# Reworking the ending of a fused state-space and attention kernel: earlier output sums, preloaded banks, a hinted branch

## The chip, the cores and the metric

One core of a Trainium2 chip, not the same chip on every occasion; every ratio compares kernels run on one chip in the same rounds. The metric is the device time of one execution in microseconds (us). Ratios are the mean time of one kernel's runs over the mean of the other's of the same rounds, so not quite the ratio of the medians that are quoted beside them. The brackets are 95% intervals.

Engines: PE is the TensorE matmul, PEld its weight load, DVE is VectorE, ACT is ScalarE, POOL is GpSimd, SP is SyncE (it issues nearly all DMAs: 167 of the 170 issues that the page of the kernel before lists, ACT the other 3).

## The reference, cut to what matters

The output is a gated mix of a complex diagonal state-space layer and 32-head attention on the same input, 2048 tokens of 1024 channels, in bf16:

```python
g = _sigmoid((x * gate_w).sum(-1, keepdims=True))
a = _A_ref(x, ...)          # h[t] = Lam_bar*h[t-1] + Bu[t];  y = 2*Re(h C) + x*Dskip
b = _B_ref(x, wqkv, wo)     # softmax(q k / sqrt(32)) v, all 32 heads, then @ wo
return g * a + (1 - g) * b
```

## The kernel before: the parts that the change touches

A scheduler in the program lays out 512 bursts. A burst computes scores (QK, 8 matmuls), gives them to two exps of 128x1024 on ACT, accumulates PV (16 matmuls) for the burst two before it, and fills the rest of PE's time with up to four matmuls of "dense" work (projections, state-space sums). Eight bursts make a unit of 256 query rows (two tiles of 128) and four heads; eight units make a head group. In the last group (bursts 448 to 511) the dense work is the output projection: 32 sums of 128x512. Each is added to a finished state-space tile, which was parked in DRAM (`ag_scratch`) and is loaded back into eight slots `Al` that reuse the memory of the input x.

```python
# the last group's sums: four partial ones of the last 256 rows, then the full ones
self.a_order = [28, 29, 30, 31] + list(range(28))
outs = [(2, self.d_out(7, r, cb, 2 * r + cb, range(7), fin=False)) for r in range(2) for cb in range(2)]
for qb in range(7):
    ...                                         # ready at burst 8*qb + 10 of the group
    outs.append((8 * qb + 10, self.d_out(qb, r, cb, k, [0, 1, 2, 3, 4, 5, 6, 7])))

for p in range(NBURST + 2):
    if p < NBURST: self.burst(p)
    if p >= 2:     self.pv(p - 2)
    ...
    if p == 448:                                # dense work has been done since burst 441
        ...                                     # load wo, part 3
        for k in range(8): ...                  # load Al[0..7] from ag_scratch

def d_out(...):                                 # sum in PSUM bank 7, then on DVE:
    scalar_tensor_tensor(o, ps[:, bank, :], gc, al, ALU.mult, ALU.add)

def tail(self):                                 # after the DMA transpose of the last unit
    for r in range(2):
        for cb in range(2):                     # one matmul and one DVE addition each
            matmul(ps[:, bank, :], OT[:, 7, ...], wo[7]..., start=True, stop=True)
            scalar_tensor_tensor(o, ps[:, bank, :], gcol, self.part[2*r+cb], mult, add)
        self.st_out(14 + r, r)
    ...                                         # range check of all 64 units, flag matmul, flag copy

def stream(name, e):                            # on each of the five engines
    S.emit(name, e, sems)                       # the whole fast path
    e.wait_ge(<flag written>)
    e.reg_load(r, flag[0:1, 0:1])
    with e.If_ne(r, 0):                         # the general path, never taken with these inputs
        ...
```

Every engine's list is one sequence, and in the traces a matmul that waits holds up the matmuls behind it. PSUM (`ps` in the code, declared as 128x8x512 f32) is what the matmuls write; one of its eight 128x512 tiles is called a bank here.

## Time and profile before

| | before |
|---|---|
| median of 3 runs, lowest to highest | 984.54 us, 984.47 to 985.25 |
| span of the profiled execution | 984.5 us (its own time: 987.31 us) |
| busy: ACT / PE / DVE | 96% / 92% / 53% |

The profiled execution is thus 2.8 us slower than the median.

From the profile page of the kernel before: busy tenths of PE and ACT in 40 slices of 24.6 us, the granted PE clock in the same slices, and the chain of work that ended last as shares of the span by engine.

```profile
span 984.5 us, 33446 instructions
...
PE   8889999999999999999999999999999999789995
...
ACT  3789999999999999999999999999999999999994
...
PEclk9999999999999999999999999999999999699998
...
ACT 88%; DVE 5%; PE 4%; DMA 2%; SPq 0%; issue 0%
```

ACT bounds the kernel: the exps hold 88% of the chain. What can be gained in the ending is what stops the exps there, and what stands after the last of them. The slice with clock 6 is around 850 us.

The timeline of ACT alone, kernel before, from 780 us on (start, duration, instructions in a row without a gap over the view's threshold; in brackets the idle time before the group and what ended it):

```profile
779.48 77.33 ACT L1431 ACTIVATE f_pt<-f_ps 128x1024 bf16<-128x1024 f32 x84
857.60 1.94 ACT L1431 ACTIVATE f_pt<-f_ps 128x1024 bf16<-128x1024 f32 x2 [0.80 <-PE f_ps L1425]
859.93 14.77 ACT L1431 ACTIVATE f_pt<-f_ps 128x1024 bf16<-128x1024 f32 x16 [0.39 <-PE f_ps L1425]
875.14 95.70 ACT L1431 ACTIVATE f_pt<-f_ps 128x1024 bf16<-128x1024 f32 x104 [0.44 <-PE f_ps L1425]
```

The exps pause at 857.6 and 859.9 because PE's scores (L1425) are late. Why they are late is seen in the windows of the same kernel (busy time of each engine and its number of instructions, then the granted clock, the DMA share and GB/s):

```profile
839.20:842.60 3.40, 1.80 (x48) 1.17 (x48) 0.02 (x2) 3.40 (x5) 0.00 (x0) 1.00 0.29 80
842.60:859.70 17.10, 12.48 (x206) 6.03 (x207) 0.91 (x4) 16.14 (x18) 0.00 (x0) 0.50 0.39 132
```

With no dense work PE was busy for 1.80 of 3.40 us, then its clock was halved for 17.1 us (column PEclk: 0.50). In the clock records every stretch at one clock that ends within the span is a multiple of 3.41 us: at half clock 3.41 (the shortest, at 13.17 us before) and 17.07 us (this one). So the clock is laid out below in windows of 3.4 us. PE was not idle in the one just before the drop: it was busy for 53% of it (1.80 of 3.40 us).

The chain of waits of the kernel before, from the last exps on (start, duration, what):

```profile
958.00 12.84 ACT f_pt L1431 x14
...
970.89 0.38 PE f_ps L1447 x8
...
971.29 0.22 DVE f_rc L1460
...
972.00 2.28 DMA f_OT<-f_On
...
974.32 0.40 PE f_ps L1641
...
974.75 1.14 DVE f_xT L1646 x2
...
976.07 1.40 DVE f_xT L1646 x2
...
979.15 0.18 PE f_ps L1664
979.33 0.02 issue
979.35 0.15 DVE flag L1666
```

After the last exp (970.83): last PV, reciprocal, a DMA transpose of 2.28 us, four matmuls and four additions one after another, the range check, the flag at 979.50. The view ends there, since branches aren't counted as work. The trace's records go on: a compare-and-branch at 980.03 to 980.11 on every engine, the next instruction of any engine only at 983.63 to 984.00, and instruction-fetch DMAs that start at 980.95 to 981.14 in between; then the closing barrier to 984.53. The last output store had landed at 979.51.

### The profile page before, as it was taken

To read this page: it belongs to the slowest core of one execution; us is meant where nothing else is said; L and a number is where in the kernel's file an instruction comes from. 1 tells how busy PE (TensorE), PEld (TensorE's weight loads), DVE (VectorE), ACT (ScalarE), POOL (GpSimd) and SP (SyncE) were. 2 spreads that over 40 slices of the span, in tenths; PEclk is the share of its full clock that TensorE was granted. 3 is DMA by queue.
4 is the path that set the end of the run, shared out by engine and by line. 5 is a ranking of instruction groups with operands and counts; after the bars stand their busy time and mean duration, and the time that the engine had idled before them with its cause. 6 is when DMAs were issued, how large, how long until landed. Compare 5 with 4: busy or idle time off the path is not lost.

```text
span 984.5 us, 33446 instructions
## 1 busy us (share of the span) xinstructions
PE 908.1 (92%) x15204; PEld 490.7 (50%) x15426; DVE 518.6 (53%) x1193; ACT 943.3 (96%) x1030; POOL 8.4 (1%) x46
## 2 busy tenths in 40 slices
PE   8889999999999999999999999999999999789995
PEld 5544554554444464444645544445544456344442
DVE  4897889877778844411267711187753112122223
ACT  3789999999999999999999999999999999999994
POOL 2000000000000000000000000000000000000000
PEclk9999999999999999999999999999999999699998
DMA  9982312311135202120023111152101210334321
GB/s 208 182 133 51 42 24 50 62 26 39 41 68 103 50 5 50 38 71 29 19 37 82 30 35 41 39 91 49 29 7 48 82 50 5 104 89 124 104 79 64
DMA packets 157302, 60.99 MB, mean 62 GB/s; under 512 B 145888, under 2 KB 145888, under 8 KB 157152
## 3 DMA queue, kind: packets, MB, share of 16 engines
q1 hardware_dynamic: 153952, 57.96, 26.8%
q8 instruction: 123, 2.02, 0.9%
q10 hardware_dynamic: 3200, 0.80, 0.4%
q14 instruction: 27, 0.22, 0.1%
HBM read 16.79 MB, written 12.58 MB: 30 GB/s over the span
## 4 chain that ended last, share of the span: by engine, by line
ACT 88%; DVE 5%; PE 4%; DMA 2%; SPq 0%; issue 0%
ACT f_pt L1431 88%; PE f_ps L1301 1%; DMA f_OT<-f_On 1%; DVE f_OT L1206 1%; PE f_ps L1425 1%; DVE f_OT L1202 1%; PE f_ps L1447 1%; DVE f_OT L1204 1%; DMA f_xT<-in_A_x_dram 1%; PE f_ps L1386 1%; SPq L1008 0%; DVE f_OT L1203 0%; PE f_ps L1283 0%; DVE f_V L1307 0%; PE f_ps L1332 0%
## 5 line engine op out<-in xcount | busy, mean ns | idle before, releaser
L1431 ACT ACTIVATE f_pt<-f_ps 128x1024 bf16<-128x1024 f32 x1024 | 941.0, 1251 | 16.9 <-PE f_ps L1425 16.8
L1447 PEld LDWEIGHTS f_ps<-f_V,f_pt 128*128 128x128 bf16 x8192 | 239.1, 96 | 111.2 <-issue 106.8
L1447 PE MATMUL f_ps<-f_V,f_pt 128*128 128x33 bf16 x8192 | 291.6, 178 | 0.8 <-DVE f_On L1461 0.5
L1425 PE MATMUL f_ps<-f_Q,f_K 32*128 32x256 bf16 x4096 | 206.0, 276 | 26.3 <-ACT f_pt L1431 8.2
L1425 PEld LDWEIGHTS f_ps<-f_Q,f_K 32*128 32x128 bf16 x4096 | 61.0, 92 | 241.7 <-ACT f_pt L1431 233.0
L1332 PE MATMUL f_ps<-f_xT,f_wb 128*128 128x512 bf16 x448 | 117.2, 377 | 13.6 <-DVE f_Q L1290 2.4
L1283 PE MATMUL f_ps<-f_xT,f_wb 128*128 128x512 bf16 x434 | 113.6, 379 | 9.0 <-issue 2.1
L1371 DVE TENSOR_SCALAR f_Ag<-f_ps,f_gcol 128x512 f32<-128x512 f32 x32 | 24.0, 751 | 139.8 <-PE f_ps L1356 139.8
L1232 DVE TENSOR_TENSOR_SCAN f_ht<-f_pf,f_init,f_ut 128x512 bf16<-128x512 f32 x64 | 80.4, 1273 | 0.0
L1356 PE MATMUL f_ps<-f_cT_im,f_hp 128*128 128x512 bf16 x192 | 72.6, 378 | 6.0 <-DVE f_Ag L1371 2.9
L1336 DVE CAST f_ub<-f_ps 128x512 bf16<-128x512 f32 x64 | 44.2, 691 | 51.9 <-PE f_ps L1332 51.8
L1301 PE MATMUL f_ps<-f_wb,f_xT 128*128 128x128 bf16 x1024 | 68.6, 222 | 0.0
L1386 PE MATMUL f_ps<-f_wb,f_OT 128*128 128x512 bf16 x220 | 59.3, 385 | 5.9 <-DVE f_xT L1396 2.0
L1301 PEld LDWEIGHTS f_ps<-f_wb,f_xT 128*128 128x128 bf16 x1024 | 59.1, 99 | 0.4 <-issue 0.2
L1332 PEld LDWEIGHTS f_ps<-f_xT,f_wb 128*128 128x128 bf16 x512 | 40.5, 96 | 35.9 <-issue 4.3
L1283 PEld LDWEIGHTS f_ps<-f_xT,f_wb 128*128 128x128 bf16 x496 | 39.2, 96 | 34.5 <-issue 1.4
L1396 DVE SCALAR_TENSOR_TENSOR f_xT<-f_ps,f_gcol,f_xT 128x512 bf16<-128x512 f32 x28 | 21.0, 751 | 64.6 <-PE f_ps L1386 64.6
L1356 PE MATMUL f_ps<-f_cT_re,f_hp 128*128 128x512 bf16 x144 | 54.4, 378 | 0.0
L1290 DVE CAST f_Q<-f_ps 128x512 bf16<-128x512 f32 x31 | 21.4, 691 | 51.3 <-PE f_ps L1283 51.3
L1223 DVE TENSOR_TENSOR f_tq<-f_ub,f_Et 128x512 bf16<-128x512 bf16 x128 | 46.3, 418 | 0.1
L1223 DVE TENSOR_TENSOR f_tq<-f_ht,f_Et 128x512 bf16<-128x512 bf16 x128 | 46.3, 417 | 0.0
L1307 DVE CAST f_V<-f_ps 128x512 bf16<-128x512 f32 x32 | 22.2, 694 | 43.2 <-PE f_ps L1301 43.2
(102 smaller groups left out, 420.1 us busy)
## 6 DMA issues: line engine op xcount, KB each, us to landing
ag_scratch<-f_Ag SPq DMA_DIRECT2D x32, 256.0 KB, 2.0
f_xT<-ag_scratch SPq DMA_DIRECT2D x32, 256.0 KB, 2.7
f_wb<-in_B_wqkv_dram SPq DMA_DIRECT2D x21, 256.0 KB, 4.2
out_dram<-f_xT SPq DMA_DIRECT2D x16, 256.0 KB, 2.3
f_OT<-f_On SPq DMA_TRANSPOSE x64, 2.4
f_wb<-in_B_wo_dram SPq DMA_DIRECT2D x1, 1024.0 KB
f_wb<-in_B_wqkv_dram ACTq DMA_DIRECT2D x3, 256.0 KB, 4.4
f_wb<-in_B_wo_dram SPq DMA_DIRECT2D x1, 768.0 KB, 4.9
```

What stands on the lines that cost most here:

```text
L1223: ops.append((c, lambda: dve(lambda e: e.tensor_tensor(o, a, b, op), r, w)))
L1232: ops.append((1.25, lambda ri=ri: dve(lambda e: e.tensor_tensor_scan(ht[:, ri, :], rr, ut[:, ri, :], self.init[:, ri, j:j + 1], ALU.mult, ...
L1283: mms.append((1, lambda e, f, l, a=a: e.matmul(ps[:, bank, :], w[:, g % 2, part, a, :], xT[:, a, 512 * ch:512 * (ch + 1)], start=f, stop=l ...
L1301: m = e.matmul(ps[:, bank, 128 * q:128 * (q + 1)], xT[:, a, 128 * kt:128 * (kt + 1)], w[:, g % 2, 2, a, :], start=(a == 0), stop=(a == 7))
L1332: mms.append((1, lambda e, f, l, a=a: e.matmul(ps[:, 7, :], bT[:, n % 2, ri, a, :], xT[:, a, 512 * ch:512 * (ch + 1)], start=f, stop=l), [ ...
L1336: self.dve(lambda e: e.tensor_copy(self.ub[:, n % 2, ri, :], ps[:, 7, :]), [("bank", 7)], [("ub", n % 2, ri)], "evac_u")
L1356: mms.append((1, lambda e, f, l, j=j, ri=ri: e.matmul(ps[:, 7, :], hp[:, ri, j, cols], cT[ri][:, j, 512 * cb:512 * (cb + 1)], start=f, sto ...
L1371: self.dve(lambda e: e.tensor_scalar(a, ps[:, 7, :], self.gcol[:, 0, tt:tt + 1], None, ALU.mult), [("bank", 7), "g0"], [at], "evac_c")
L1386: mms.append((1, lambda e, f, l, j=j: e.matmul(ps[:, bank, :], OT[:, j, 256 * qb + 128 * r:256 * qb + 128 * (r + 1)], wo[j][0][:, 512 * cb ...
L1425: m = e.matmul(ps[:, 2 * sl[h // 2] + h % 2, 256 * kl:256 * (kl + 1)], K[32 * h:32 * h + 32, g % 2, 128 * kt:128 * (kt + 1)], Q[32 * h:32 ...
L1431: self.act(lambda e, s=s, p=p: e.activation(pt[:, p], ps[:, 2 * s:2 * s + 2, :], ACT.Exp, scale=SCALE), [("S", s)], [("pt", p)], "exp")
L1447: m = e.matmul(ps[:, 6, o:o + 33], pt[:, p, h2, 256 * kl + 128 * qt:256 * kl + 128 * (qt + 1)], V[:, g % 2, 2 * i + kl, h, :], start=(i == ...
```

## The change

Intent: start the output projection as soon as the dense work runs out (burst 442), so that the clock isn't dropped; make the end after the last exp short: no DMA transpose, no serial additions, most of the check done earlier, and no instruction fetch behind the branch. A branch hint is an instruction of its own, placed some way ahead of the branch that it belongs to.

```diff
+        rcb = [(r, cb) for r in range(2) for cb in range(2)]
+        seq = [(442, 6, r, cb, "part") for r, cb in rcb] + [(450, 7, r, cb, "part") for r, cb in rcb]
+        for qb in range(6):
+            seq += [(458 + 8 * qb, qb, r, cb, "full") for r, cb in rcb]
+        seq += [(506, 6, r, cb, "rest") for r, cb in rcb]
...
-        for p in range(NBURST + 2):
+        for p in range(NBURST):
...
-            if p == 448:
+            if g >= 6 and not last and not proj[7] and not us and not cs and cur is None and not self.bg:
+                last = True                     # loads of wo part 3 and of Al[0..7] follow
...     # partial sums of the last 256 rows are kept as a bf16 pair hi + lo
+            if kind == "part" and qb == 7:
+                add(su, al, alt, ...); tensor_copy(hi, su); tensor_tensor(lo, su, hi, ALU.subtract)
...     # tail: put them back into PSUM by identity matmuls, and let the last product add to them
+        check(0, 63, 0, 63, 0)
+        self.pv(NBURST - 2)
+        preload(0)
+        self.pv(NBURST - 1, (0,))
+        preload(1)
+        self.pv(NBURST - 1, (1,))
+        ...     # reciprocal; two halves normalised, transposed on PE, copied by ACT
+        check(63, 64, 63, 65, 2)
+        ...     # 4 tail matmuls with start=False, the flag matmul after the first two
+        ...     # plain copies to bf16, two on ACT and two on DVE, and two stores
...
+    MARK_AT = dict(pe=64, act=24, dve=40, pool=1, sp=16)    # operations before the end of the stream
...
-                with e.If_ne(r, 0):
+                br = e.br_cmp(r, 0, on_true="done_" + name, on_false="bad_" + name, comp_op="IS_EQ")
+                br.branch_hint(loc[0])          # loc: marked MARK_AT operations before the end
```

## The prediction

> **What bounds it now.** ScalarE's exp stream: by the chain that ended last it holds 88% of the span; 1024 exps start 0.914 us apart (instructions in order of time), waiting for PE only 16.8 us in all (the waits). The change touches none of that. It aims at the 13.7 us from the end of the last exp (970.84) to the end of the span (984.5). In order of time these are: last PV, reciprocal, normalise (to 971.98); a DMA transpose of 2.3 us to 974.3; four tail matmuls feeding four 0.74 us DVE additions in a row (to 977.47); the check and flag, 2.0 us, to 979.50; register load 0.5 us; a compare-and-branch after which no engine does anything for 3.5 us (980.09 to 983.6, with two instruction-fetch DMAs inside it); then semaphore waits and the closing barrier, 0.9 us. The last output store had landed by about 979.2, so everything after that is flag and branch.
>
> A second loss: between bursts 441 and 449 PE has no dense work (838 to 855 us, PE 50 to 70% busy by stretches) and its clock is granted only 0.5 from 842.6 to 859.7. The first output sums then run at half clock and the exps lose 1.2 us in idle, 1.7 us by the spacing of their starts.
>
> **What changes.**
> 1. Partial sums start at burst 442 instead of 450. The dense gap shrinks to one period, so this clock drop should vanish: -1.7 us. But the first sum must wait for its scratch load, which landed around 843.7; PE has almost no slack before the next QK: about +0.4.
> 2. Last unit: the DMA transpose (2.3) becomes two PE transposes and two ScalarE copies of 128x128 (estimate 0.3 each from 0.60 for 128x512 and 0.20 for 128x8), pipelined with a split normalise: about 1.2.
> 3. The four additions become two ScalarE and two DVE copies in parallel.
> 4. Check: 63 of 64 units are checked early, but the short remainder (about 1.2 us of 0.16 to 0.3 us pieces) precedes DVE's copies, and the flag matmul stands before the last two tail matmuls.
> 5. The store becomes last (1.7 us from issue to landing), overlapped with register load and branch.
> 6. Branch hint: the 3.5 us should fall to some 0.1. [...]
> 7. Cost: eight 512-column preload matmuls stand among the last PVs; at 0.215 us each the second four delay the last PV by about 0.4 us.
>
> **The risk.** From burst 507 to 511 PE carries one dense matmul per burst or none. [...] in this trace mere 50% occupancy did it. I expect the half clock again (chance 0.7), and then preloads and tail take twice as long: about +2.3 us.
>
> **Sum.** With the clock whole, last exp to end is about 7.3 us instead of 13.7: -6.4; mid-kernel -1.2: 976.9. With the half clock 979.3. Hint failing: up to +2.5, chance 0.15. Mean about 978.5. Range 975.8 to 981.5. Faster by over 2% (under 965) is out of reach: 0.01; slower 0.005.
>
> **What would show it.** No half clock and no ScalarE idle at 842 to 860; branch under 0.3 us on all engines; no DMA transpose after the last exp; matmul spacing of the preloads 0.215 or 0.43 us; last to land is the final output store; last exp about 1.2 us earlier.
>
> **What would make it wrong.** The hint not taking, or hurting the straight instruction stream; [...] the first sums stalling exps more; late transposes at bursts 459 and 491 (now 0.4 us each) growing.

Three passages are cut from it, because no trace of this case shows what they say: what makes a branch stall, what makes the clock halve ("did it", in what is left of "The risk", means that the clock halved: after the window with PE busy for 1.80 of 3.40 us), and an item of the last list that presumes a threshold of the clock. 984.5 - 6.4 - 1.2 is the 976.9, and 2.3 more for the half clock the 979.3 (979.2 by the rounded terms). Two figures are estimates: the 0.1 us of step 6 (in the trace before the compare-and-branch records of ACT, DVE, POOL and SP last 0.05 to 0.07 us, and the 3.5 us stand behind them), and the 2.3 us of the half clock (matmuls of 512 columns start 0.215 us apart there at whole clock and 0.43 at half).

## The result, and the profile after

| first set, same chip | before | after |
|---|---|---|
| median, lowest to highest | 984.50 us, 983.89 to 985.25 (4 runs) | 982.49 us, 980.73 to 983.78 (4 runs) |
| ratio | | 0.9978 [0.9960, 0.9996] |

The change is a little faster, and 1.0 us outside the predicted range. Repeated on another chip (run e5 below) the ratio was 0.9955.

The page of the kernel after, the same rows as before:

```profile
span 982.1 us, 33717 instructions
...
PE   7889999999999999999999999999999999899996
...
ACT  4789999999999999999999999999999999899996
...
PEclk9999999999999999999999999999999999899997
...
ACT 87%; PE 5%; DVE 5%; DMA 1%; SPq 1%; issue 0%; DVEq 0%
```

The low clock in the 35th slice is nearly gone, but ACT has lost a tenth in that very slice. To see the sums, the two spans are cut at the same exps (times of starts, from the records of the two traces):

| stretch | before, us | after, us | difference |
|---|---|---|---|
| start to exp 64 (code unchanged) | 87.69 | 85.88 | -1.81 |
| exp 64 to 832 (bursts 32 to 416, unchanged) | 704.64 | 704.62 | -0.02 |
| exp 832 to 1008 (bursts 416 to 504) | 163.46 | 165.74 | +2.28 |
| exp 1008 to end of the last | 15.05 | 15.31 | +0.26 |
| last exp to end of span | 13.70 | 10.50 | -3.20 |
| span | 984.53 | 982.06 | -2.47 |

The start-up difference is put down to the run and not to the change: the code there is the same, and it lies between 85.6 and 87.7 us in the profiles told here. So in these two profiles the change bought 3.2 us at the end and gave 2.5 us back before it.

ACT's timeline after, from 780 us on:

```profile
779.54 64.44 ACT L1447 ACTIVATE f_pt<-f_ps 128x1024 bf16<-128x1024 f32 x70
847.65 1.94 ACT L1447 ACTIVATE f_pt<-f_ps 128x1024 bf16<-128x1024 f32 x2 [3.66 <-PE f_ps L1441]
850.04 112.04 ACT L1447 ACTIVATE f_pt<-f_ps 128x1024 bf16<-128x1024 f32 x122 [0.46 <-PE f_ps L1441]
962.29 9.27 ACT L1447 ACTIVATE f_pt<-f_ps 128x1024 bf16<-128x1024 f32 x10 [0.21 <-PE f_ps L1441]
```

The small pauses of before are gone, but there is one of 3.66 us at 847.65, when the first output sums run. All engines in that stretch of the kernel after, cut to the lines that matter:

```profile
839.27 4.71 SPq L1572 DMA_DIRECT2D f_xT<-ag_scratch  x8
...
844.35 0.75 DVE L1401 SCALAR_TENSOR_TENSOR f_xT<-f_ps,f_gcol,f_xT 128x512 f32<-128x512 f32 x1 [6.95 <-DMA f_xT<-ag_scratch]
...
845.16 1.89 PE L1395 MATMUL f_ps<-f_wb,f_OT 128*128 128x512 bf16 x4 [2.97 <-DVE f_xT L1401]
...
846.98 0.61 PE L1441 MATMUL f_ps<-f_Q,f_K 32*128 32x256 bf16 x8
```

Read it downwards. The load of the first state-space tile is issued at 839.27 (SPq). The first sum is ready long before, but its addition on DVE starts only at 844.35, released by that load. The second sum needs the same PSUM bank, so its first matmul stands on PE for 2.97 us, and the scores of the next burst (L1441) stand behind it in PE's order until 846.98. ACT has nothing to do in the meantime.

The windows of the kernel after: around this pause, and around the second drop of the clock.

```profile
841.80:848.60 6.80, 3.83 (x46) 1.59 (x43) 0.75 (x1) 3.14 (x5) 0.00 (x0) 0.63 0.91 302
959.70:963.10 3.40, 2.15 (x46) 1.24 (x42) 1.16 (x2) 3.19 (x4) 0.00 (x0) 1.00 0.32 101
963.10:972.00 8.90, 7.58 (x119) 3.68 (x119) 3.44 (x9) 8.46 (x10) 0.00 (x0) 0.50 0.16 61
```

In the first, the mean clock is 0.63: half clock for 6.83 us from 843.61, a result of the pause (PE was busy for 1.71 us of the 3.40 before it; in e3, without the pause, the clock stays whole there). In the last, half clock from 963.08 for 10.24 us: bursts 506 to 511 have one dense matmul or none. The chain of waits of the kernel after, from there:

```profile
970.50 1.71 PE f_ps L1665 x4
972.21 0.23 PE f_ps L1463 x8
972.44 1.36 PE f_ps L1665 x4
973.80 0.21 PE f_ps L1463 x8
...
974.03 0.22 DVE f_rc L1675
974.25 0.02 issue
974.27 0.37 DVE f_On L1678 x2
...
974.69 0.24 PE f_ps L1681
...
974.96 0.29 ACT f_OT L1684
...
976.54 0.14 DVE flag L1704
```

The eight preload matmuls (L1665) stand between the last PVs (L1463), so the reciprocal starts at 974.03, 2.47 us after the last exp (971.56); before it was 0.46 us. From the reciprocal to the flag it takes 2.65 us (before: 8.2), as meant. The rest is in the records of branches, fetches and landings:

| after the flag, us after the last exp | before | after |
|---|---|---|
| flag written | 8.67 | 5.12 |
| last store issued | 6.67 | 5.79 |
| last of its 16 parts landed (us after its issue) | 8.68 (2.01) | 9.63 (3.84) |
| branch to next instruction: PE | 3.54 | 0.55 |
| the same: ACT / DVE / POOL / SP | 3.87 / 3.89 / 3.77 / 3.63 | 2.66 / 3.65 / 3.33 / 2.90 |
| SP past its branch | 12.84 | 9.62 |
| end of span | 13.70 | 10.50 |

Two things were unexpected. Only PE's branch became short; an 8 KB instruction fetch for each of the other four still ran about 1 us after its branch. And the last store became slow: 12 of its 16 parts landed within 2.04 us of the issue, the other four after 2.53, 2.90, 3.58 and 3.84 us, while these fetches ran. The store's end (981.19) and SP's next instruction (981.18) came at the same moment.

One thing the profile doesn't cover: the reported time is longer than the span, by 1.7 to 1.8 us in all runs of the kernel after, but by 2.8, 3.5 and 3.3 us (means of 11 runs on each later occasion) in those of before. So part of the gain lies after the span's end. In the profile of before one more instruction fetch is recorded 2.7 us after the end of the span; the one of after has none. The same went together in e1 and e6 below (fetch 2.0 and 2.2 us after the end, differences of 2.46 and 2.28 us), and e12, without hints but without such a fetch either, has 1.75. The two go together in the profiles; as a cause it was not isolated.

### The profile page after: what moved, and what is told of

Same layout as the page of the kernel before. It is cut to its first block, busy times and chain, and to the rows that moved or that the text cites. A ratio compares the mean times of both kernels' runs of the same rounds, so it can differ in the third digit from the quotient of the medians.

```text
span 982.1 us, 33717 instructions
## 1 busy us (share of the span) xinstructions
PE 938.0 (96%) x15436; PEld 489.8 (50%) x15436; DVE 524.9 (53%) x1210; ACT 944.9 (96%) x1034; POOL 8.4 (1%) x46
## 4 chain that ended last, share of the span: by engine, by line
ACT 87%; PE 5%; DVE 5%; DMA 1%; SPq 1%; issue 0%; DVEq 0%
ACT f_pt L1447 87%; PE f_ps L1463 1%; PE f_ps L1395 1%; PE f_ps L1441 1%; DVE f_OT L1214 1%; PE f_ps L1309 1%; DVE f_OT L1210 1%; DVE f_OT L1212 1%; DMA f_xT<-ag_scratch 1%; SPq L1016 0%; PE f_ps L1291 0%; DVE f_OT L1211 0%; DMA f_xT<-in_A_x_dram 0%; PE f_ps L1340 0%; DVE f_V L1315 0%
## 5 line engine op out<-in xcount | busy, mean ns | idle before, releaser
L1463 PEld LDWEIGHTS f_ps<-f_V,f_pt 128*128 128x128 bf16 x8192 | 239.7, 96 | 110.5 <-issue 106.4
L1463 PE MATMUL f_ps<-f_V,f_pt 128*128 128x33 bf16 x8192 | 291.9, 179 | 0.5 <-DVE f_On L1477 0.5
L1441 PE MATMUL f_ps<-f_Q,f_K 32*128 32x256 bf16 x4096 | 205.2, 275 | 23.1 <-ACT f_pt L1447 4.9
L1441 PEld LDWEIGHTS f_ps<-f_Q,f_K 32*128 32x128 bf16 x4096 | 61.0, 93 | 240.9 <-ACT f_pt L1447 231.5
L1340 PE MATMUL f_ps<-f_xT,f_wb 128*128 128x512 bf16 x512 | 131.0, 378 | 4.1 <-DVE f_Q L1298 2.4
L1291 PE MATMUL f_ps<-f_xT,f_wb 128*128 128x512 bf16 x496 | 127.4, 380 | 2.3 <-DVE f_V L1315 1.3
L1364 PE MATMUL f_ps<-f_cT_re,f_hp 128*128 128x512 bf16 x192 | 72.8, 379 | 0.3
L1395 PE MATMUL f_ps<-f_wb,f_OT 128*128 128x512 bf16 x252 | 67.9, 388 | 4.7 <-DVE f_xT L1401 3.0
L1401 DVE SCALAR_TENSOR_TENSOR f_xT<-f_ps,f_gcol,f_xT 128x512 bf16<-128x512 f32 (+1 forms) x32 | 24.0, 751 | 71.5 <-PE f_ps L1395 64.5
```

The costliest lines, as they stand in the source:

```text
L1291: mms.append((1, lambda e, f, l, a=a: e.matmul(ps[:, bank, :], w[:, g % 2, part, a, :], xT[:, a, 512 * ch:512 * (ch + 1)], start=f, stop=l ...
L1340: mms.append((1, lambda e, f, l, a=a: e.matmul(ps[:, 7, :], bT[:, n % 2, ri, a, :], xT[:, a, 512 * ch:512 * (ch + 1)], start=f, stop=l), [ ...
L1364: mms.append((1, lambda e, f, l, j=j, ri=ri: e.matmul(ps[:, 7, :], hp[:, ri, j, cols], cT[ri][:, j, 512 * cb:512 * (cb + 1)], start=f, sto ...
L1395: mms.append((1, lambda e, f, l, j=j: e.matmul(ps[:, 7, :], OT[:, j, 256 * qb + 128 * r:256 * qb + 128 * (r + 1)], wo[j][0][:, 512 * cb:51 ...
L1441: m = e.matmul(ps[:, 2 * sl[h // 2] + h % 2, 256 * kl:256 * (kl + 1)], K[32 * h:32 * h + 32, g % 2, 128 * kt:128 * (kt + 1)], Q[32 * h:32 ...
L1463: m = e.matmul(ps[:, 6, o:o + 33], pt[:, p, h2, 256 * kl + 128 * qt:256 * kl + 128 * (qt + 1)], V[:, g % 2, 2 * i + kl, h, :], start=(i == ...
```

## The experiments

The theory, as it stood in the end: the gain is lost in four places; the third was formed on the result of e2. (1) The first sums' scratch tile comes too late, and PE's order hands the wait on to the exps. (2) The hint does nothing on four engines, because it stands behind the last block of instructions that these engines fetch. (3) The branch's fetches delay the last store. (4) The order of the preloads delays the last PV. Rivals: the half clock at the end rather than the order costs the time in (4); hints don't work on these engines at all; the dense sums at burst 442 are no gain in themselves.

Eleven kernels and the change once more were run on three occasions (e1 to e4, e5 to e8, e9 to e12), all with five rounds, all with correct results. Medians, and ratios to the kernel before on the same chip and rounds (its medians: 985.83, 986.73 and 985.92 us, 11 runs each):

| run | median, us (runs) | ratio | pause at bursts 444 to 447 | reciprocal after last exp | last exp to end |
|---|---|---|---|---|---|
| before (first profile) | | | 0 | 0.46 | 13.70 |
| after (first profile) | | | 4.64 | 2.47 | 10.50 |
| e1 | 983.98 (6) | 0.9982 [0.9967, 0.9997] | 1.04 | 1.96 | 10.32 |
| e2 | 982.69 (6) | 0.9971 [0.9956, 0.9986] | 2.51 | 2.85 | 10.79 |
| e3 | 980.68 (5) | 0.9950 [0.9937, 0.9963] | 0 | 1.83 | 9.94 |
| e4 | 982.69 (6) | 0.9974 [0.9957, 0.9992] | 1.44 | 1.95 | 10.16 |
| e5 | 982.21 (6) | 0.9955 [0.9939, 0.9971] | 2.58 | 2.22 | 10.29 |
| e6 | 983.92 (5) | 0.9974 [0.9961, 0.9987] | 0 | 0.46 | 13.87 |
| e7 | 977.50 (5) | 0.9918 [0.9904, 0.9931] | 0 | 0.46 | 8.52 |
| e8 | 976.67 (4) | 0.9906 [0.9891, 0.9921] | 0 | 0.46 | 7.24 |
| e9 | 982.79 (6) | 0.9959 [0.9944, 0.9974] | 4.42 | 1.15 | 9.74 |
| e10 | 982.32 (5) | 0.9960 [0.9947, 0.9973] | 4.56 | 2.69 | 9.47 |
| e11 | 976.38 (4) | 0.9906 [0.9892, 0.9921] | 0 | 0.46 | 7.25 |
| e12 | 980.20 (5) | 0.9943 [0.9930, 0.9956] | 0 | 0.46 | 10.47 |

The last three columns are from the one profile of each run. The pause is by how much the starts of the exps there fall behind their usual spacing of 0.914 us; ACT's idle time alone is shorter (in the change 4.12 us of the 4.64).

### e1: the change without its hints

```diff
-                br.branch_hint(loc[0])
```

> The changed kernel with the five branch hints taken away (the hint call on the branch dropped, the branch itself unchanged). In the changed kernel's profile only PE's branch was short (0.49 us, next instruction at 977.83); ACT, POOL, DVE and SP each stood 2.7 to 3.7 us after theirs and each had an instruction fetch about 1 us after the branch, as in the kernel before. Theory (the hints did nothing on the engines that end last, because they stand behind the last fetch of a new block on these engines): same time as the changed kernel within 0.7 us, PE's branch now 3.5 us too, SP's wait unchanged at 2.9 us. Rival (the hints help, and the end would be worse without them): 1.5 us or more slower than the changed kernel.

PE's branch took 4.42 us to its next instruction (0.55 with the hint); the other four 2.99 to 3.74, as with the hint. From the last exp to the end it took 10.32 us against 10.50: the hints of the change bought nothing within the span, since only PE's works and PE isn't the last.

### e2: hints further ahead

In the change ACT, DVE, SP and POOL execute the hint at 950.8, 911.7, 920.2 and 557.2 us; the last instruction block that ACT, DVE and SP fetch in the straight stream comes at about 882, 857 and 650 us, POOL fetches none. PE executes its hint at 953.0 and fetches again at 954.8. Here the hints of ACT, DVE and SP go ahead of that last fetch; POOL's stream is lengthened by no-ops.

```diff
-    MARK_AT = dict(pe=64, act=24, dve=40, pool=1, sp=16)
+    MARK_AT = dict(pe=64, act=170, dve=150, pool=1, sp=130)
...
+            if name == "pool":
+                for _ in range(160):
+                    e.nop()
```

> The changed kernel with the hints of ACT, DVE and SP 130 to 170 operations before the end instead of 16 to 40, so that each engine's last fetch of a new instruction block (seen at 882, 857 and about 650 us) comes after its hint; POOL gets 160 no-operation instructions after its hint for the same reason. Theory (a hint acts at the next fetch after it): ACT, DVE, SP and POOL leave the branch in under 0.7 us with no instruction fetch of theirs after it, and the end then waits for the last store, about 979.5 to 980.5 in the changed kernel's time: 1.0 to 2.0 us faster than the changed kernel. Rival (these engines with their smaller blocks can't use the hint at all): branches stay at 2.7 to 3.7 us, time unchanged within 0.7 us.

ACT, DVE and SP now go on 0.49, 0.60 and 0.53 us after their branch, like PE; POOL still takes 2.80 us (the no-ops left no trace). So the rival that hints don't work on these engines falls, and the place of the hint is what matters. Its lead in time alone doesn't do it: POOL's hint ran 418 us ahead of its branch. But the end came no earlier: 10.79 us after the last exp. SP passed its branch at once and then waited for the last store, four parts of which landed 2.69, 3.26, 3.57 and 3.88 us after the issue, with fetches still started at 977.2 to 978.2. The branch and the store had ended together; removing one uncovers the other.

### e3: the first four scratch tiles loaded about 11 us earlier

Against the same exps, the first load is issued 10.8 us earlier than in the change (the expectation says 5). The tiles go into columns of x that the dense work stops reading earlier, so that the load needn't wait for the last of it.

```diff
-        self.Al = [self.xT[:, t, 1024:2048].bitcast(F32) for t in range(8)]
+        self.Al = [self.xT[:, t, 0:1024].bitcast(F32) for t in range(4)] + [self.xT[:, t, 1024:2048].bitcast(F32) for t in range(4, 8)]
...     # the partial sums swap places with them
+            if g >= 6 and not first4 and len(proj[7]) <= 2 and not cs and cur is None:
+                first4 = True                   # load Al[0..3]
```

> The changed kernel with the first four scratch tiles loaded to the x columns that are free about 5 us earlier (tokens 0 to 1023; the four partial sums go to the others), so the first sum's addition at burst 443 need not wait for its load. Theory (ScalarE's 4.1 us of idle at 847 to 850 comes from the second sum's wait for the bank, held by an addition that waits for a load): the PE wait of 3.0 us at burst 444 is gone, no half clock at 844 to 850, ScalarE idle there under 0.3 us, 3.5 to 4.5 us faster than the changed kernel. Rival (the period without dense work at burst 441 halves the clock anyway and the half clock makes the loss): a clock of 0.5 stays near 843 to 850 and the gain is under 2 us.

The timeline of ACT in e3, where the pause was:

```profile
778.94 180.00 ACT L1447 ACTIVATE f_pt<-f_ps 128x1024 bf16<-128x1024 f32 x196
959.20 9.27 ACT L1447 ACTIVATE f_pt<-f_ps 128x1024 bf16<-128x1024 f32 x10 [0.26 <-PE f_ps L1441]
```

196 exps in a row: no pause, and no half clock at 843. Bursts 416 to 504 take 161.39 us (before 163.46, after 165.74). It is the best of the four on this chip: 2.0 to 3.3 us by the medians under e1, e2 and e4, which keep the wait (less than the 3.5 to 4.5 expected; e5's ratio is from another chip and is no base for it). Its runs lie within 1.5 us, those of the three within 4.5 to 5.5 us. That fits the load's latency scattering the change's times, but the kernel before, without this wait, scatters by 3.2 us on the same occasion, and why was not looked into.

### e4: PE kept busy at the end

Three filler matmuls ahead of each lone one in bursts 506 to 509, four in 510 and 511.

```diff
+        if kind == "rest":
+            fill = lambda e, f, l: e.matmul(ps[:, 7, :], OT[:, 0, 0:128], wo[0][0][:, 512:1024], start=True, stop=True)
+            mms = [(1, fill, ...)] * 3 + [<the real one>]
+        for p in (510, 511): ...                # four fillers each
```

> The changed kernel with matmuls whose result nobody reads put into bursts 506 to 511 (three before each lone matmul, four in each of the last two bursts), so that PE's load per burst stays that of the bursts before. Theory (the thin last bursts halve the clock and the preloads then run at 0.43 us each, holding the last PV): no clock of 0.5 between 960 and the last exp, preload spacing about 0.215 us, last exp to end 10.5 us falls to about 8, gain 1.5 to 2.8 us. Rival (the preloads' place before the last PV, not the clock, holds the end up): gain under 0.7 us.

The clock stayed whole to 975.99, and the preloads ran 0.215 us apart instead of 0.43. Yet the reciprocal still came 1.95 us after the last exp, and the end 10.16 us after it, where about 8 had been expected. The half clock is not the main cost; what stands ahead of the last PV in PE's order is (here that includes the four fillers of burst 511, so e9 and e11 test it without them).

### e5: the change again, on the chip of the next three

No edit.

> The changed kernel itself once more, on the same chip as the three that follow, as their base. Theory: about 0.9975 of the kernel before, single runs spread over 4 us or more because the wait at burst 444 differs from run to run (1.0 to 4.1 us of ScalarE idle in the four profiles that have that part unchanged), against 2 us for the kernel with the early loads. Rival (the spread comes from the start-up or the ending): the spread stays in the kernels with early loads too.

0.9955 here, 0.9978 in the first set: the change gains between 0.2 and 0.5%. The means of the spans fell from 982.99 to 980.17 us, the means of the times from 986.46 to 981.94; the other 1.7 us lie after the span's end. Single runs spread by 4.6 us. The pause was 2.58 us, the half clock at the end the same 10.24 us (from 960.84).

### e6: the kernel before, with fillers alone in the gap

```diff
+            if 441 <= p <= 449 and cur is None:
+                ...                             # four filler matmuls, results not used
```

> The kernel before with four matmuls per burst whose result nobody reads in bursts 441 to 449, where PE had no dense work; nothing else. Theory (the half clock from 842.6 to 859.7 made the first sums slow and ScalarE idle 1.7 us): no clock of 0.5 there, ScalarE gaps at bursts 443, 450 and 451 gone, 1.2 to 1.9 us faster than the kernel before. Rival (the first sums wait for data, not the clock): gaps at 450 and 451 stay, gain under 0.5 us.

The window in which before had half clock, in e6:

```profile
841.00:858.00 17.00, 16.21 (x260) 7.62 (x257) 1.39 (x4) 17.00 (x20) 0.00 (x0) 1.00 0.42 143
```

The clock is whole (1.00), ACT is busy throughout, and bursts 416 to 504 take 161.71 us instead of 163.46: 1.75 us less, where 1.7 had been predicted for this step. (The mean span fell by 1.4 us; the rest of the total's 2.6 us lies after the span's end.) Keeping PE busy is worth what was said; fillers that compute nothing get it, without the early sums and their wait.

### e7: the remedies together

Early loads as in e3; hints ahead of the last fetch on all engines, with 150 real (tiny) memsets on POOL in place of no-ops; the "rest" sums at burst 507, because at 506 the first waited 1.23 us for its transpose; fillers in bursts 506 to 510 as in e4; the second preload behind the last PV.

```diff
+        for _ in range(150):
+            self.pool(lambda e: e.memset(self.padn[:], 0.0), [], ["padn"])
...
         self.pv(NBURST - 1, (0,))
-        preload(1)
         self.pv(NBURST - 1, (1,))
+        preload(1)
...
-    MARK_AT = dict(pe=64, act=24, dve=40, pool=1, sp=16)
+    MARK_AT = dict(pe=64, act=170, dve=150, pool=154, sp=130)
```

> The changed kernel with all remedies but one: early loads of four scratch tiles; hints ahead of the last block fetch on every engine (POOL gets 150 memsets of one column after its hint, since no-operations left no trace on POOL); the last sums of rows 1536 to 1791 one burst later (507), so the transpose of their last piece is there; fillers in bursts 506 to 510; the second four preload matmuls behind the last PV instead of ahead of it. Theory, by the profiles: no ScalarE gap over 0.3 us after burst 440, last PV within 0.4 us of the last exp's end (2.1 us in the changed kernel), branch under 0.7 us on all five engines, last exp to end 8.0 to 9.0 us, total 4 to 6 us under the changed kernel. Rival (hints and order gain nothing because the last store's landing ends the kernel whatever comes before it): last exp to end above 9.5 us.

977.50 us, no pauses, the reciprocal 0.46 us after the last exp, all five branches at most 0.60 us (POOL too: its stream now has a fetch behind the hint). The end is the late store: its last parts landed 3.13, 3.29, 3.60 and 4.01 us after the issue, while fetches ran at 971.49 to 972.36 although no engine waited for them.

### e8: e7, and every engine waits for the last store before its branch

```diff
                 e.reg_load(r, flag[0:1, 0:1])
+                e.wait_ge(sems[fast.last_store.lane], 16 * fast.last_store.tick)
                 br = e.br_cmp(...)
```

> The same as the previous one, but each engine waits for the last store to land before it branches. In the changed kernel 12 of the last store's 16 parts landed within 2.0 us of its issue and 4 only 2.5 to 3.8 us after, while the instruction fetches of the branch ran; in the kernel before, with no fetch at that time, all 16 were there after 2.0 us. Theory (the fetches delay the store): all 16 parts land within 2.1 us of the issue, branch after it, end within 1 us of the landing, time equal or up to 1 us better than the previous one. Rival (the store is late for another reason): 4 parts still late, and the end 0.7 us or more later than in the previous one.

All 16 parts landed within 2.05 us of the issue, since the fetches now come at 974.2, 1 us after the branch. The end is 7.24 us after the last exp, 1.28 us less than in e7: a wait was added, and the end came earlier. PE's timeline in e8 at the last PV:

```profile
967.33 0.37 PE L1468 MATMUL f_ps<-f_V,f_pt 128*128 128x33 bf16 x8 [0.36 <-ACT f_pt L1452]
967.55 1.02 PE L1682 MATMUL f_ps<-f_Et,f_ident 128*128 128x512 bf16 x4
968.41 0.49 PE L1698 MATMUL f_ps<-f_ident,f_On 128*128 128x128 bf16 x2
```

The last PV (L1468) now waits only for the last exp (which ends at 967.28), and the preload (L1682) runs while DVE normalises.

### e9: the change, with only the second preload behind the last PV

```diff
-        preload(1)
         self.pv(NBURST - 1, (1,))
+        preload(1)
```

> The changed kernel with one line moved: the second four preload matmuls stand behind the last PV instead of ahead of it. In the two profiles of the changed kernel the reciprocal of the last unit started 2.5 us after the last exp's end, in the kernel before 0.46 us. Theory (PE works in order, so preloads ahead of a PV hold it): the reciprocal starts 0.5 to 1.3 us after the last exp's end (the first four preloads can still be in the way at half clock), last exp to end about 9.3 us against 10.3 to 10.5, 0.5 to 1.5 us faster than the changed kernel's 0.9955 of the kernel before, within its spread. Rival (the half clock alone is the matter): no change of the reciprocal's distance over 0.3 us.

The reciprocal comes 1.15 us after the last exp, 1.3 us sooner than in the change, at the same half clock (963.15 to 973.4). With whole clock (e7, e8) it is 0.46. PE's timeline in e9 shows what the other 0.7 us is:

```profile
970.32 1.87 PE L1665 MATMUL f_ps<-f_Et,f_ident 128*128 128x512 bf16 x4
971.98 0.67 PE L1463 MATMUL f_ps<-f_V,f_pt 128*128 128x33 bf16 x16
```

The first four preloads run at half clock and hold the last sixteen PV matmuls until 971.98, 0.45 us after the last exp (971.53). So of the 2.0 us that the change lost here, 1.3 is the order, and 0.7 the half clock under the first preloads. The sizes are of single profiles: in the seven with the change's order of preloads the reciprocal came 1.83 to 2.85 us after the last exp. The expected gain in total, 0.5 to 1.5 us, does not show (0.9959 against e5's 0.9955): it is lost in the noise of the pause (4.42 us in this profile). And the end is only 0.76 us nearer, because the earlier tail now falls partly into the half clock (reciprocal to flag 3.07 us, in the change 2.65) and the store lands a little later (its last part: 4.11 us).

### e10: the change, with working hints and the wait for the store

The hints and POOL's memsets of e7 and the wait of e8, nothing else.

> The changed kernel with working hints on all five engines (placed ahead of the last block fetch, 150 memsets on POOL) and with each engine waiting for the last store before it branches; nothing else. Theory (branch fetches and the last store's landing are the two things that end the kernel): landing of all 16 parts within 2.1 us of the issue, end about 1.4 us after it, last exp to end about 9.0 us, 1.0 to 1.6 us less than in the changed kernel. Rival: last exp to end stays over 10 us.

All parts within 2.05 us, all branches within 0.60 us. The end comes 9.47 us after the last exp, although the reciprocal comes 0.22 us later than in the change. From the issue of the store to the end it takes 3.46 us (e8: 3.46) where the change took 4.71: these two remedies together are worth 1.25 us. Neither is worth anything alone: with hints and no wait it takes 4.62 us (e2) and 4.75 us (e7), with the wait and no hints 6.69 us (e12). The total hides it behind a pause of 4.56 us.

### e11: e8 without any fillers

> The fastest kernel so far (all remedies, branch after the store) without the fillers in the last bursts, everything else the same. Theory: a clock of 0.5 comes back between 958 and 970, last exp to end 0.4 to 1.2 us longer than 7.2 us, total 0.4 to 1.2 us slower. Rival (with the second preloads moved, the half clock no longer touches the chain): within 0.3 us.

0.9906, the same as e8, with half clock from 959.03 for 6.83 us: that drop ended (965.86) before the last PV (966.84), and nothing waited for it. The slowdown that had been expected did not come, so the fillers aren't needed here. This rests on where the drop falls: in e9, where it lasted to 973.4, it did hold the first preloads. This is the best version, and the simplest of those that reach it.

### e12: e8 without the hints

```diff
-                br.branch_hint(loc[0])
```

> The fastest kernel so far without the branch hints, everything else the same. Theory: with the branch behind the last store its 3 to 3.9 us of fetch is laid bare: last exp to end 9.8 to 11 us against 7.2, 2.6 to 3.7 us slower. Rival (hints are worth little wherever they stand): under 1 us.

10.47 us from the last exp to the end, 3.2 more than e8 and e11, with all branches at 3.35 to 4.30 us. So a hint is worth 3.2 us of span once the branch stands behind the store, where nothing else is left to hide it.

## Why the prediction was wrong, point by point

**Right.** The exps' steady state was untouched (704.64 and 704.62 us). Keeping PE busy from burst 442 on is worth 1.7 us by itself (e6: 1.75). The half clock at the end came. The transpose, the serial additions and the late check went about as costed (reciprocal to flag 8.2 us before, 2.65 after; a copy of 128x128 on ACT took 0.29 us, estimated 0.3). The best case, 7.3 us from the last exp to the end, is reached by e8 and e11 (7.24 and 7.25), though not by the change. That the number fits so well is luck: it was put together from a store that overlaps the branch, and in e8 and e11 the branch follows the store.

**Wrong, first and largest: "the first sum must wait for its scratch load, which landed around 843.7; PE has almost no slack before the next QK: about +0.4".** The wait was named and mis-sized. In the seven profiles with this part as the change has it the pause was 1.04 to 4.64 us, mean 3.0. The landing time was taken from the old trace, where the loads weren't awaited and the first tile was complete 3.12 us after its issue. In the changed kernel the last of its 16 parts landed 3.0 to 5.0 us after the issue, differing by run. In e1, e4 and e2 (landing +3.01, +3.41, +4.50; pause 1.04, 1.44, 2.51) the pause is this time less 2.0 us: all that exceeds the slack reaches ACT, since PE works in order. In the other four (e5 +3.58, 2.58; e10 +4.62, 4.56; e9 +4.76, 4.42; after +4.98, 4.64) it is 1.0 to 1.9 us more, and there, and only there, the clock halved again at the pause. So "this clock drop should vanish" failed with it in four of seven. By the same 2.0 us of slack, the landing that the prediction took (843.7, 2.6 us after the old issue at 841.08) would have made a pause of 0.6 us: the slack was about right, the landing and the half clock that came back were mis-sized. e3 takes the wait away and gains the whole stretch. What makes the tile late was not isolated. In the change one part of 16 is late (15 are there after 2.93 us); the tile competes with seven other loads (DMA share 0.91 in that window); a 16 KB instruction fetch of PE's ran just then, but it did so in e1 too, where the tile was not late.

**Wrong, second: "Branch hint: the 3.5 us should fall to some 0.1", with a chance of 0.15 of failing.** It fell to 0.55 us, on PE alone; the other four stayed at 2.66 to 3.65 us. In all cases without a working hint the next instruction came 2.66 to 4.42 us after the branch; in the change each of these four branches had an 8 KB fetch behind it. A hint worked here only if a block of the straight stream was still fetched after it (e2; POOL in e7; down to 0.47 to 0.60 us).

**Not foreseen, third: the fetches of the branch delay the store.** "The store becomes last (1.7 us from issue to landing), overlapped with register load and branch" was the step: the last part landed 3.84 us after the start of the issue, 2.01 by the same count in the kernel before. Just 4 of 16 parts were late while the fetches ran, and none was late when the fetches came after the store (e8, e10, e11, e12; in e8 and e10 all 16 within 2.05 us). By what means the fetches hold the packets up was not shown. The packets agree: in the change 11 of the last two stores' 256 packets of 2 KB took over 0.12 us, up to 0.53, all between 978.1 and 980.4, about when the branch's fetches ran (978.27 to 980.10); the median packet took 0.09. In the other seven profiles with such an overlap 9 to 14 packets were slow, in the six without it none took over 0.11 us. On which DMA engine a packet ran is not in the kept records.

**Fourth: the order of the preloads.** "The second four delay the last PV by about 0.4 us", and twice that and the tail at half clock "+2.3". The reciprocal came 2.0 us later than before relative to the last exp: 1.3 by the order at half clock, 0.7 by the clock (e9, e8). The order was under-sized and the clock over-sized: it was whole again at 973.32, before the reciprocal at 974.03, so the tail did not take twice as long.

The sums: with the half clock foreseen the prediction was 979.3 us. In the profiles the bursts to the last exp came out 3.7 us above it (+2.54 instead of -1.2), the end 0.9 us above (10.50 instead of 7.3 + 2.3), the start-up 1.81 us below: together 2.8 above, a span of 982.06 us. That the start-up was short was luck in the prediction's favour. These are spans; the prediction took the old span for the time. In times it forecast -5.2 us (984.5 to 979.3), and the medians fell by 2.0. The end: 10.50 in the change and 7.24 in e8 differ by 3.26 us, of which 2.01 are the reciprocal's delay and 1.25 hints and store.

**Left open.** Why the reported time exceeds the span by more in most kernels without hints; why the first tile's last part is late; and what in PE's activity makes the clock halve (last section).

## What to carry to other kernels

Work that is moved forward is only as early as its data: where an engine works in order, as PE did here (a late tile cost the exps 1.04 to 4.64 us), check when each input lands, with its scatter, and start the loads earlier first. In an ending, list everything that finishes last together (here store and branch), since removing one of two that end at the same moment was worth nothing here (e2); and don't put idle-time work ahead of the instruction that the chain waits for (1.3 us here, e9). In this kernel a branch hint worked ahead of the last instruction block that the engine fetches, and the branch belonged behind the last store; only both together gained (1.25 us, e10).

## What the runs show of branches, fetches and the clock

- A branch hint that stood ahead of a later block fetch made the step from branch to next instruction 0.47 to 0.60 us on all five engines; one that stood behind the last fetch left it at 2.66 to 3.65 us (run of the change), much as without a hint (3.54 to 3.89 in the kernel before).
- ACT, DVE, POOL and SP fetched 8 KB of instructions at a time, by the counts between fetches 128 instructions, and only PE 16 KB (sizes in the DMA records; in the page of before, queue q14 with 27 packets and 0.22 MB, and q8 with 123 and 2.02 MB).
- The compare-and-branch itself lasted 0.045 to 0.084 us in the records of ACT, DVE, POOL and SP (before and after), but the next instruction came no sooner than 0.47 us after its start, and without a working hint up to 4.4 us.
- Instruction fetches behind a branch held up the last output store: four of its 16 parts landed 0.5 to 2.3 us later than the rest in all eight profiles where both overlapped, none in the six where they didn't.
- The clock halved after windows in which PE was far from idle. Those of 3.4 us in which PE was busy for 1.80 us (53%, 842.6 us before) and for 2.15 us (63%, 963.1 us after) were followed by half clock, one with 3.27 us (e6) was not. Laid out by the clock's steps of 3.41 us, the windows at whole clock from 800 to 970 us in all 14 profiles give this: all eight in which PE was busy for 40 to 55% were followed by half clock, none over 64% was, and of nine from 58 to 63% five were and four weren't. So busy time alone does not decide it.
- Whether no-ops count as instructions to be fetched was not shown: 160 of them on POOL left no record, brought no further fetch and left its branch at 2.80 us (whether they were in the stream at all was not checked); 150 tiny memsets brought two fetches (558.4 and 578.2 us in e7) and 0.48 us.
